# Four u parts, three dense PSUM banks, single PV banks, ScalarE copies and a new ordering model in a two-layer attention and token-MLP kernel

## The chip, the cores and the metric

The kernel runs on one core of one Trainium2 chip. The metric is the device time of one execution in microseconds (us), lower is better; a time quoted is the median of several executions. Each run has a state, fast or slow; ratios below use fast runs alone.

Engine names: PE is TensorE (matmuls; PEld its weight loads), DVE is VectorE, ACT is ScalarE, POOL is GpSimd, SP issues DMAs. L802 is line 802 of the kernel that the line belongs to. Lines shift between kernels, so the same code is L643 in one and L672 in another.

## The reference, cut to what matters

Two equal layers. Each is sliding-window attention (2048 tokens, 32 heads of 16, window 256) and then an MLP across tokens (2048 to 1792 and back), both with LayerNorm and a residual.

```python
x = A_x
for layer in range(2):                      # unrolled in the original
    x = x + attention(layernorm(x))         # softmax over the last 256 keys; qkv and output projection
    h = layernorm(layernorm(x))             # x is [tokens, 512]
    u = gelu(w1.T @ h + b1)                 # [1792, 512], contraction over all 2048 tokens
    x = x + w2.T @ u + b2
```

The contraction of u runs over tokens. So u can be accumulated in token parts of 512, as soon as attention has finished a part. The next layer's first matmuls need y = w2.T @ u, hence all of u.

## The kernel before

The kernel is a graph of operations. A greedy scheduler written in Python orders it before the launch: it keeps a model of time for each engine, always places the operation that can start first, and so fixes the instruction order of every engine. Operations carry a cost and a latency to their readers. PSUM (in the kernel 8 banks of 128x512 fp32) is a pool with a limit for each class: "sc" for scores, "small" for dense groups and PV results during attention.

```python
class Graph:
    def op(self, eng, fn, reads=(), writes=(), cost=100.0, lat=60.0, ...):  # 60 ns to any reader
    ...
    def _pick(self, e, cand, ready, free, mode):
        ...
        for o in cand:
            t = max(ready[o.idx], free)
            if e == "tensor" and o.mode != mode:
                t += SWITCH                        # 95 ns
            ...   # while a PV result is due within HOLD, no dense group may take a small bank
    HOLD = 1500.0
    WINDOW = {0: 250.0, 1: 150.0}                  # a score (0) or PV (1) goes first if it can start this soon
    def schedule(self):
        ...
        o.end = free[e] = m + o.cost
        o.done = o.end + o.lat                     # 200 ns for PE operations, also towards PE itself
        ...
        ready[u.idx] = max(ready.get(u.idx, 0.0), o.done)
```

```python
psum = Pool("psum", 8, {"sc": 6, "small": 2, "big": 6})
...
# in attention: five pieces for each of 4 head groups; a piece needs two score pairs (4 banks)
sa, sb_ = Tile(psum, 2, "sc"), Tile(psum, 2, "sc")
...                                                # scores on PE, exp on ACT (two 128x1024), mask on DVE
tO = Tile(psum, 2, "small")                        # PV result: a pair of banks
...
op("vector", f_ev, ...)                            # cs <- both banks, one copy of 128x1024
...
# in qkv: every copy out of PSUM (xhT, qT, stg, vt) is on "vector"
...
prepare(0, "big"); prepare(1); tos[0] = attention(0, ...); prepare(2); wo_block(0, tos[0])
tos[1] = attention(1, ...); prepare(3); wo_block(1, tos[1]); u_part([0, 1], True, False)
tos[2] = attention(2, ...); wo_block(2, tos[2]); u_part([2], False, False)
tos[3] = attention(3, ...); wo_block(3, tos[3], "big"); u_part([3], False, True)
```

`prepare` makes LayerNorm, q, k and v of a token part and, in the second layer, first the y blocks of the first. `wo_block` is the output projection with the LayerNorms that follow.

The softmax here doesn't subtract the row's maximum and nothing guards it: scores larger than these inputs give would overflow.

## Time and profile before

The time was 535.56 us (three runs, 534.03 to 537.4). From the page of the kernel before: the engines (busy us, share of the span, instructions) and the busy tenths in 40 equal slices; PEclk is the granted TensorE clock in tenths.

```profile
span 536.2 us, 15441 instructions
...
PE 443.4 (83%) x6754; PEld 208.6 (39%) x6816; DVE 375.9 (70%) x726; ACT 307.0 (57%) x340; POOL 135.1 (25%) x205
...
PE   2979767687688789899989878888779899699997
...
ACT  0555698888999810421784997588767921051000
...
PEclk9979998897999999999999999999988999989999
...
```

No engine is busy all the time.

ACT's timeline of the kernel before around its holes (start us, length us, then the work; in brackets the idle time before it and what ended it):

```profile
...
26.92 7.01 ACT L655 ACTIVATE pt<-PS 128x1024 bf16<-128x1024 f32 x8 [0.51 <-PE PS L643]
42.81 7.11 ACT L655 ACTIVATE pt<-PS 128x1024 bf16<-128x1024 f32 x8 [8.88 <-PE PS L688]
56.65 1.94 ACT L655 ACTIVATE pt<-PS 128x1024 bf16<-128x1024 f32 x2 [6.73 <-PE PS L688]
```

Three lines of PE's timeline near the end of the second layer: u of part 2 (L802), 14 matmuls of the last output projection (L763), then a 5.07 us hole until LayerNorm has made `xh_sb`, and u of part 3, with the clock cold at first (granted 0.50 from 467.6 to 474.4 us).

```profile
...
448.98 12.46 PE L802 MATMUL PS<-xh_sb,w1b 128*128 128x512 bf16 x55
461.27 3.19 PE L763 MATMUL PS<-wo_sb,oT 128*128 128x512 bf16 x14
469.52 14.65 PE L802 MATMUL PS<-xh_sb,w1b 128*128 128x512 bf16 x55 [5.07 <-DVE xh_sb L516]
...
```

The copy of PV results (DVE, 30 of 128x1024):

```profile
...
L731 DVE COPY cs<-PS 128x1024 f32<-128x1024 f32 x30 | 36.4, 1217 | 3.0 <-PE PS L688 2.7
...
```

### The profile page before, as it was taken

The numbers are of one execution on the slowest core, as the hardware profiler recorded it, in microseconds if no ns is written. First come the engines' busy times: TensorE is split into PE (matmuls) and PEld (weight loads), VectorE is DVE, ScalarE is ACT, GpSimd is POOL, SyncE is SP. The second block draws the span as 40 slices with busy tenths as digits, with TensorE's granted clock in tenths as the row PEclk, the third lists the DMA queues.
The fourth block names the chain that finished last, engine by engine and source line by source line (L and its number), as shares of the span: only waits on it lengthen the run. The fifth ranks groups of instructions, "written<-read, shape, count | busy, mean of one in ns | idle before, by whom it ended". The sixth has DMA issues, their size and how long they took to land.

```text
span 536.2 us, 15441 instructions
## 1 busy us (share of the span) xinstructions
PE 443.4 (83%) x6754; PEld 208.6 (39%) x6816; DVE 375.9 (70%) x726; ACT 307.0 (57%) x340; POOL 135.1 (25%) x205
## 2 busy tenths in 40 slices
PE   2979767687688789899989878888779899699997
PEld 1453432252233334344434335334434334244443
DVE  5889977786866678757789778778785657862322
ACT  0555698888999810421784997588767921051000
POOL 3525244343300120013203502712551020100000
PEclk9979998897999999999999999999988999989999
DMA  8912253242356543442255353156314662323663
GB/s 276 221 44 82 73 188 111 90 111 90 123 159 189 178 120 101 122 121 70 70 173 168 127 151 126 42 164 180 123 42 132 200 191 82 96 60 87 179 190 114
DMA packets 91435, 69.23 MB, mean 129 GB/s; under 512 B 16232, under 2 KB 79848, under 8 KB 91368
## 3 DMA queue, kind: packets, MB, share of 16 engines
q1 hardware_dynamic: 91368, 68.25, 42.8%
q8 instruction: 53, 0.87, 0.7%
q14 instruction: 14, 0.11, 0.1%
HBM read 49.42 MB, written 18.32 MB: 126 GB/s over the span
## 4 chain that ended last, share of the span: by engine, by line
PE 41%; ACT 27%; DVE 21%; issue 3%; POOL 3%; DMA 3%; SPq 0%; POOLq 0%; DVEq 0%
ACT pt L655 27%; PE PS L825 13%; PE PS L802 12%; PE PS L564 4%; PE PS L688 4%; PE PS L643 3%; DVE stats L505 3%; DVE cs L731 3%; PE PS L763 2%; DVE x_sb L767 2%; DVE pt L671 2%; DVE pt L668 2%; DVE xh_sb L516 2%; DVE stg L572 1%; PE PS L589 1%
## 5 line engine op out<-in xcount | busy, mean ns | idle before, releaser
L655 ACT ACTIVATE pt<-PS 128x1024 bf16<-128x1024 f32 (+1 forms) x304 | 280.9, 1041 | 104.0 <-PE PS L643 74.5
L802 PE MATMUL PS<-xh_sb,w1b 128*128 128x512 bf16 x431 | 107.4, 393 | 13.5 <-DVE xh_sb L516 6.7
L825 PE MATMUL PS<-ub,w2b 128*128 128x512 bf16 x428 | 101.7, 380 | 2.4 <-issue 1.3
L643 PE MATMUL PS<-qT,kbd 32*128 32x64 bf16 (+4 forms) x1632 | 62.8, 247 | 40.9 <-ACT pt L655 21.7
L671 DVE TENSOR_TENSOR pt<-pt,ldm 128x1024 bf16<-128x1024 bf16 (+1 forms) x80 | 57.2, 716 | 25.5 <-ACT pt L655 25.5
L564 PE MATMUL PS<-xhT,wqkv 128*128 128x512 bf16 x238 | 65.3, 404 | 8.1 <-DVE x_sb L767 1.5
L753 POOL TENSOR_TENSOR oT<-md 128x512 bf16<-128x512 f32 x30 | 41.2, 1375 | 111.0 <-DMA md<-rscr 111.0
L802 PEld LDWEIGHTS PS<-xh_sb,w1b 128*128 128x128 bf16 x448 | 41.2, 100 | 68.4 <-issue 10.5
L643 PEld LDWEIGHTS PS<-qT,kbd 32*128 32x128 bf16 x1632 | 23.8, 93 | 101.2 <-ACT pt L655 64.7
L825 PEld LDWEIGHTS PS<-ub,w2b 128*128 128x128 bf16 x448 | 40.7, 98 | 50.0 <-issue 5.2
L575 POOL TENSOR_SCALAR kbd<-stg,par 128x512 bf16<-128x512 bf16 x64 | 47.8, 758 | 48.8 <-DVE stg L572 48.6
L668 DVE TENSOR_TENSOR pt<-pt,ldm 128x512 bf16<-128x512 bf16 (+1 forms) x104 | 43.5, 428 | 20.2 <-ACT pt L655 19.8
L830 DVE SCALAR_TENSOR_TENSOR x_sb<-PS,b2col,x_sb 128x512 bf16<-128x512 f32 x32 | 23.0, 739 | 43.7 <-PE PS L825 43.7
L510 POOL TENSOR_SCALAR rstd<-agg 128x2 f32<-128x2 f32 (+1 forms) x36 | 9.2, 254 | 160.5 <-DVE agg L507 158.0
L817 ACT ACTIVATE ub<-ub,b1col 128x512 bf16<-128x512 f32 x28 | 18.6, 713 | 50.6 <-DVE ub L814 50.5
L814 DVE TENSOR_TENSOR ub<-PS,ub 128x512 f32<-128x512 f32 x56 | 35.9, 684 | 14.8 <-PE PS L802 14.8
L688 PE MATMUL PS<-pt,vt 64*18 64x64 bf16 (+4 forms) x3040 | 38.7, 242 | 7.5 <-DVE pt L668 2.3
L505 DVE BATCH_NORM_STATS2 stats<-x_sb 128x6 f32<-128x512 bf16 x64 | 42.6, 684 | 3.2 <-DMA x_sb<-in_A_x_dram 2.6
L731 DVE COPY cs<-PS 128x1024 f32<-128x1024 f32 x30 | 36.4, 1217 | 3.0 <-PE PS L688 2.7
L763 PE MATMUL PS<-wo_sb,oT 128*128 128x512 bf16 x121 | 34.6, 403 | 4.7 <-DVE oT L719 3.1
L564 PEld LDWEIGHTS PS<-xhT,wqkv 128*128 128x128 bf16 x256 | 22.3, 102 | 40.2 <-issue 8.9
L688 PEld LDWEIGHTS PS<-pt,vt 64*18 64x18 bf16 x3040 | 30.3, 84 | 18.4 <-ACT pt L655 5.3
(45 smaller groups left out, 316.0 us busy)
## 6 DMA issues: line engine op xcount, KB each, us to landing
scr<-cs SPq DMA_DIRECT2D x30, 512.0 KB, 3.5
w1b<-in_B_w_dram SPq DMA_DIRECT2D x56, 256.0 KB, 3.0
w2b<-in_B_w_dram SPq DMA_DIRECT2D x16, 896.0 KB, 5.9
md<-scr SPq DMA_DIRECT2D x60, 128.0 KB, 2.6
md<-rscr SPq DMA_DIRECT2D x60, 128.0 KB, 3.4
out_dram<-x_sb SPq DMA_DIRECT2D x16, 128.0 KB, 4.7
wqkv<-in_A_wqkv_dram SPq DMA_DIRECT2D x3, 512.0 KB
x_sb<-in_A_x_dram SPq DMA_DIRECT2D x3, 512.0 KB, 9.3
```

Of the source, the lines that this page charges most:

```text
L505: op("vector", lambda e, t=t: e.bn_stats(stats[:, t, :], x_sb[:, t, :]), reads=[f"x{t}"], writes=[f"st{t}"], cost=dve_cost(512))
L564: mm_group(ft, 4, lambda e, c: e.matmul(PS[:, ft.slot, :], lhsT=wqkv[:, c, which * 512 + o * P:which * 512 + (o + 1) * P], rhs=xhT[:, tx.s ...
L575: op("gpsimd", lambda e, h=h: e.tensor_scalar(kbd[:, tk[o].slot, :, h, :], stg[:, ts.slot, :].rearrange("p (s n) -> p s n", n=64), par[:, ...
L643: last = e.matmul(PS[:, bank(r), c0 * 64:(c0 + nb) * 64], lhsT=kbd[32 * r:32 * r + 32, tkk.slot, jj, :, :].rearrange("p h n -> p (h n)"), ...
L655: return e.activation(pt[:, tp.slot, 2 * u:2 * u + 2, 0:n], PS[:, b0:b0 + 2, 0:n], ACTF.Exp, scale=SMSCALE)
L668: return e.tensor_tensor(v, v, msk.unsqueeze(1).to_broadcast([P, 4, w]), op=ALU.mult)
L671: return e.tensor_tensor(v, v, msk.unsqueeze(1).unsqueeze(1).to_broadcast([P, 4, k, w]), op=ALU.mult)
L688: last = e.matmul(PS[32 * r:32 * r + 18, tO.slots[h], q0 * 64:(q0 + nb) * 64], lhsT=vt[64 * h:64 * h + 64, tvv.slot, jj, 4 * o + r, :], rh ...
L731: return e.tensor_copy(cs[:, tc.slot], PS[:, b0:b0 + 2, :])
L763: mm_group(ft, 4, lambda e, o, i=i, ft=ft: e.matmul(PS[:, ft.slot, :], lhsT=oT[:, tos[o][0].slot, i * P:(i + 1) * P], rhs=wo_sb[:, 4 if to ...
L802: out_ = e.matmul(PS[:, tu.slot, :], lhsT=w1b[:, tw.slot, s, tt * P:(tt + 1) * P], rhs=xh_sb[:, 4 * m + s, :], start=(n == 0 and s == 0), ...
L825: mm_group(ft, NFT, lambda e, fc: e.matmul(PS[:, ft.slot, :], lhsT=w2b[:, tw.slot, fc, k * P:(k + 1) * P], rhs=uT(fc), start=(fc == 0), st ...
```

## The change

The intent: more dense matmuls available for PE while ACT does exponentials (u in four parts, in the first layer only; a third dense bank), less work for DVE early (ScalarE may take the copies of token parts 0 and 1), PV banks handled one by one, and an ordering model that was meant to be closer to the chip, with a clock gate. (The gate is the rule inside the model, by which PE costs double in some stretches.) Cut to its core:

```diff
+STEPS = ("p0 p1 a0 p2 w0 u0 a1 p3 w1 u1 a2 w2 u2 a3 w3 U3",     # first layer: four u parts
+         "p0 p1 a0 p2 w0 a1 p3 w1 u01 a2 w2 u2 a3 w3 U3")       # second layer: block order as before
...
+    LAT = {"tensor": 200.0, "vector": 120.0, "scalar": 150.0, "gpsimd": 100.0, "sync": 60.0}
...
-            t = max(ready[o.idx], free)
+            t = free
             if e == "tensor" and o.mode != mode:
                 t += SWITCH
+            t = max(ready[o.idx], t)
...
-    HOLD = 1500.0
-    WINDOW = {0: 250.0, 1: 150.0}
+    HOLD = 0.0
+    WINDOW = {0: 100.0, 1: 150.0}
...
+                if e == "tensor":
+                    o.cost = self._clocked(m, o.cost)    # twice the cost where the model takes the clock for half
-                o.done = o.end + o.lat
+                o.done = o.end + (o.lat if o.lat is not None else self.LAT[e])
-                ready[u.idx] = max(ready.get(u.idx, 0.0), o.done)
+                ready[u.idx] = max(..., o.end if e == "tensor" and "tensor" in u.engs else o.done)
...
-        psum = Pool("psum", 8, {"sc": 6, "small": 2, "big": 6})
+        psum = Pool("psum", 8, {"sc": 6, "small": 3, "big": 6})
...
+                if m < NACT:                              # NACT = 2, both layers
+                    engs["scalar"] = (lambda e: e.copy(dst(), src()), act_cost(512))
...
-                tO = Tile(psum, 2, "small")
+                tO = [Tile(psum, 1, "small") for _ in range(2)]
...
-                op("vector", f_ev, reads=[tO], writes=[tc], cost=dve_cost(1024, psum=True), prio=-1e5)
+                for h in range(2):
+                    op("vector", ... e.tensor_copy(cs[:, tc.slot, h], PS[:, tO.slot, :]) ..., cost=dve_cost(512, psum=True))
```

Two costs in the model changed as well (LayerNorm scaling 320, the POOL multiply 1680). A switch that was never used (`apart`) went out.

## The prediction

> **What bounds the kernel now.** No single engine: PE is busy 83%, DVE 70%, ACT 57% of 536.2 us (engine table); the chain of waits is PE 41%, ACT 27%, DVE 21%. By stages (10 us windows):
>
> - 20-60 us, first layer: DVE is busy 38 of 40 us with PSUM copies, LayerNorm, masks. ACT, which owes the exponentials, has holes at 33.9-42.8 and 49.9-56.7 us.
> - 60-190 us: ACT is busy 116 of 130 us with exponentials (1052 ns each for 128x1024). PE is busy only 75%: dense work has run out. The u matmuls (L802) start at 144 us, since u of token parts 0 and 1 is one block after the second output projection.
> - 187-230 us: exponentials are over; PE does most of u of part 2 (until 218 us), the last output projection, then u of part 3.
> - 230-440 us, second layer: PE 80-90% busy, because y of the first layer fills it; a 5.1 us PE hole at 464 us before the last u.
> - 484-532 us: y, dense, untouched.
>
> The granted clock is half in stretches (27-37, 82-85, 102-106, 122-130, 399-406, 467-475 us), some 34 us in all; at 469 us an L802 matmul shows 634 ns instead of 379. [...]
>
> **What the change does.**
>
> 1. First layer's u in four parts: the 56 matmuls of part 0 (0.219 us spacing in dense stretches, 12 us) can run from about 105 us, in the holes and cold clock of the exponential stage. Price: 14 more DVE adds of 684 ns, 9.6 us. Some 10 us of u leave 187-219 us; the last projection and LayerNorm chain stays, about 20 us by my estimate. Net gain 6-9 us.
> 2. Early copies may go to ScalarE: up to 64 (token parts 0 and 1, both layers). DVE pays 0.41-0.68 us each. I expect 20-40 to move, at 0.6 us (Ln of 128x512 from PSUM takes 600 ns). At 20-60 us, 12-16 moved copies take 7-10 us off the saturated DVE: 5-8 us gained. In the second layer PE is the limit: 1-3 us.
> 3. PV banks copied singly: two copies near 0.68 us replace one of 1217 ns, 30 x 0.15 = 4 us more DVE work, mostly hidden; a bank comes free about 0.6 us earlier. PE waited 8.2 us for this copy, plus 14.1 us at weight loads: 2 us gained.
> 4. A third dense bank overlaps dense evacuation, but leaves score pairs five banks at times. About zero.
> 5. Order by the clock model: fewer half-clock windows in the first layer. 2-4 us. The hole at 464 us may stay, since the second layer keeps its block order.
>
> DMA bytes and the y stage stay. The terms overlap; sum some 16 us.
>
> **Prediction:** 519 us, 8 in 10 between 506 and 533. Chances: faster by over 2% 0.68, within 2% 0.28, slower 0.04.
>
> **What the profile would show.** Copies on ACT before 60 us and its two holes halved; last exponential of the first layer near 180 us, not 187; L802 from about 105 us; y starting near 218, not 230 us; mean clock at least 0.97; 60 cs copies; DVE busy near 370 us, ACT near 325. The second layer shortens by only 3-6 us.
>
> **What would make it wrong.** DVE becoming the limit at 105-190 us through the extra adds; ACT copies landing between exponentials where ACT is the limit; the third dense bank starving scores (ACT waiting for L643 more than 74.5 us); cold windows falling elsewhere. Better than predicted: the new order closing the second layer's holes too.

The five terms as they stand add up to 16 to 26 us (6-9, 5-8 and 1-3, 2, 0, 2-4). The 2 to 4 us of term 5 are the author's estimate: no trace shows what order does to the granted clock. The "about 20 us" of term 1 can be checked: in the trace of before, the last output projection of the first layer goes on at 199.50 us and u of part 3 starts at 219.52 us.

## More of the kernel before

The stages show more. The next answer gives the busy time of each engine in stretches: 20 us to 60 us; to the last exponential of the first layer (187.4 us); to its last gelu (231.3 us); to the first exponential of the second layer (251.0 us); to its last (432.1 us); to the last gelu (485.8 us), after which only y is left. The columns after the engines are the granted clock, the DMA share and GB/s.

```profile
...
core 0: us, PE busy (x) PEld busy (x) DVE busy (x) ACT busy (x) POOL busy (x), PEclk, DMA share, GB/s
20.00:60.00 40.00, 33.70 (x504) 19.72 (x508) 38.12 (x95) 22.67 (x27) 17.47 (x27) 0.91 0.36 100
60.00:187.40 127.40, 94.55 (x2332) 44.18 (x2346) 94.37 (x161) 116.18 (x126) 38.39 (x47) 0.95 0.44 136
187.40:231.30 43.90, 39.72 (x279) 18.00 (x284) 34.54 (x67) 11.65 (x18) 4.78 (x9) 1.00 0.42 116
231.30:251.00 19.70, 19.49 (x111) 9.11 (x112) 11.18 (x24) 1.30 (x2) 4.54 (x11) 1.00 0.38 105
251.00:432.10 181.10, 152.80 (x2972) 72.27 (x2995) 139.47 (x269) 140.34 (x152) 57.12 (x76) 0.98 0.42 128
432.10:485.80 53.70, 46.25 (x299) 20.13 (x302) 35.65 (x65) 11.93 (x18) 4.92 (x9) 0.94 0.34 97
...
```

Until 60 us DVE is full (38.1 of 40 us) and ACT is not (22.7). To 187 us ACT is full (116.2 of 127.4 us) and PE is not (94.6). In the second layer's exponential stage (251 to 432 us) PE is busy 152.8 of 181.1 us, so 28.3 us of it are idle.

From the groups by line in 251 to 432 us of the kernel before, the score matmuls (after the second bar: idle time of PE just before them, with what ended it):

```profile
...
L643 PE MATMUL PS<-qT,kbd 32*128 32x320 bf16 (+4 forms) x808 | 30.5, 244 | 16.1 <-ACT pt L655 9.3 <-DVE cs L731 2.0 <-POOL kbd L575 0.9
...
```

And three lines of PE's timeline within that stage (L825 is y):

```profile
...
306.73 0.40 PE L643 MATMUL PS<-qT,kbd 32*128 32x128 bf16 x12 [0.46 <-ACT pt L655]
307.06 1.04 PE L825 MATMUL PS<-ub,w2b 128*128 128x512 bf16 x4
...
400.95 2.34 PE L802 MATMUL PS<-xh_sb,w1b 128*128 128x512 bf16 x5 [1.78 <-ACT pt L655]
...
```

PE stood idle before score matmuls, 9.3 us in this stage, until an exponential had freed their banks. Dense work existed: at 307.06 us y comes right behind such scores, with no wait of its own. Not every hole is of that kind: at 400.95 us a dense matmul of u, L802, waited 1.78 us for an exponential itself, so there a free bank was missing too.

## The result, and the profile after

The kernel after took 503.1 us (three runs, 501.5 to 506.04). Ratios here are the mean time of one kernel's fast runs over that of the other's of the same rounds, so not quite the ratio of the quoted medians. The ratio to before is 0.940 (95% interval 0.932 to 0.948): faster, as forecast, but by 32 us instead of 16, and outside the stated range. The page of the kernel after:

```profile
span 499.8 us, 15471 instructions
...
PE 430.5 (86%) x6746; PEld 209.0 (42%) x6816; DVE 377.1 (75%) x745; ACT 321.9 (64%) x365; POOL 137.0 (27%) x205
...
PE   2998758798859859699999899898889998999997
...
ACT  1788987898789961080598998697988872070000
...
PEclk9999988899979979899999999999999999999999
...
```

Its stages, cut at the same events (last exponential of the first layer at 182.4 us, last gelu 223.1, first exponential of the second layer 242.3, last 410.7, last gelu 450.0):

```profile
...
core 0: us, PE busy (x) PEld busy (x) DVE busy (x) ACT busy (x) POOL busy (x), PEclk, DMA share, GB/s
20.00:60.00 40.00, 35.18 (x686) 20.38 (x688) 39.23 (x97) 36.00 (x46) 17.49 (x24) 1.00 0.50 144
60.00:182.40 122.40, 93.18 (x2143) 44.76 (x2156) 101.00 (x185) 107.00 (x115) 39.12 (x50) 0.92 0.43 136
182.40:223.10 40.70, 34.63 (x244) 15.88 (x249) 27.65 (x49) 12.63 (x18) 3.16 (x5) 0.90 0.34 99
223.10:242.30 19.20, 19.09 (x108) 8.96 (x109) 12.28 (x24) 2.97 (x5) 4.74 (x11) 1.00 0.39 108
242.30:410.70 168.40, 154.50 (x3003) 74.88 (x3034) 140.42 (x278) 144.63 (x159) 58.22 (x76) 1.00 0.47 146
410.70:450.00 39.30, 36.36 (x267) 17.24 (x271) 32.29 (x62) 11.97 (x18) 4.81 (x9) 1.00 0.36 101
...
```

| stretch | before, us | after, us | gained, us |
|---|---|---|---|
| start to last exponential, first layer | 187.4 | 182.4 | 5.0 |
| to last gelu, first layer | 43.9 | 40.7 | 3.2 |
| to first exponential, second layer | 19.7 | 19.2 | 0.5 |
| to last exponential, second layer | 181.1 | 168.4 | 12.7 |
| to last gelu, second layer | 53.7 | 39.3 | 14.4 |
| y to the end | 50.4 | 49.8 | 0.6 |

The profiled runs differ by 36.4 us, the medians by 32.5. The first layer gained 8.2 us, where the prediction had 11 to 17 us from its first two terms. The second layer, whose block order the change leaves as it was, gained 28.2 us, where it had 3 to 6. That is more than the whole miss. (One stretch of this table needs care: of the 14.4 us after the last exponential of the second layer, about 7 are luck of the order of before, see "Luck of the order".)

In the second layer's exponential stage PE is busy about the same time as before (154.5 and 152.8 us) but in 168.4 us instead of 181.1: its idle time fell from 28.3 to 13.9 us (some records of matmuls are missing in both traces, 62 of 6816 before and 70 after, so PE's idle time is a little too high in both). The score matmuls of that stage, to compare with the line of before:

```profile
...
L672 PE MATMUL PS<-qT,kbd 32*128 32x320 bf16 (+4 forms) x808 | 29.7, 243 | 3.1 <-DVE qT L567 1.1 <-DVE vt L567 1.0 <-POOL kbd L604 0.7
...
```

Idle time before them fell from 16.1 to 3.1 us. What the profile puts down to exponentials fell from 9.3 us to nothing listed. At the end of the second layer, the lines that answer to the three of before:

```profile
...
419.20 2.54 PE L791 MATMUL PS<-wo_sb,oT 128*128 128x512 bf16 x11 [1.29 <-DVE oT L748]
...
422.87 11.39 PE L830 MATMUL PS<-xh_sb,w1b 128*128 128x512 bf16 x51
...
438.41 4.49 PE L830 MATMUL PS<-xh_sb,w1b 128*128 128x512 bf16 x19 [1.13 <-DVE xh_sb L541]
...
```

Here 11 matmuls of the last projection (L791) come before the 51 of u (L830). LayerNorm is done while those run, the hole is 1.13 us instead of 5.07, and the clock stays up (granted 1.00 over the stretch, where before had 0.94). (Before with one constant of its model moved by 2 ns loses that hole as well: 1.46 us.) The end of the first layer of the same kernel still has the poor order, projection after u, with a hole of 4.87 us:

```profile
...
193.10 7.07 PE L830 MATMUL PS<-xh_sb,w1b 128*128 128x512 bf16 x31
200.00 3.19 PE L791 MATMUL PS<-wo_sb,oT 128*128 128x512 bf16 x14
208.06 7.97 PE L830 MATMUL PS<-xh_sb,w1b 128*128 128x512 bf16 x30 [4.87 <-DVE xh_sb L541]
```

The ScalarE copies (25 of 64 moved) and the PV copies of the kernel after, from the groups by shape (busy us, mean ns):

```profile
...
L569 ACT COPY xhT<-PS 128x512 bf16<-128x512 bf16 x8 | 4.5, 590 | 19.2 <-PE PS L579 19.2
...
L569 ACT CAST qT<-PS 128x512 bf16<-128x512 f32 x7 | 4.1, 585 | 1.7 <-PE PS L595 1.7
L569 ACT CAST vt<-PS 128x512 bf16<-128x512 f32 x5 | 3.0, 598 | 0.0
L569 ACT CAST stg<-PS 128x512 bf16<-128x512 f32 x5 | 3.0, 592 | 3.6 <-PE PS L595 3.6
...
```

```profile
...
L759 DVE COPY cs<-PS 128x512 f32<-128x512 f32 x60 | 38.5, 682 | 6.4 <-PE PS L717 6.2
...
```

### The profile page after: what moved, and what is told of

The parts are those of the page before. It is cut to its first block, busy times and chain, and to the rows that moved or that the text cites. A ratio compares the mean times of both kernels' runs of the same rounds, so it can differ in the third digit from the quotient of the medians.

```text
span 499.8 us, 15471 instructions
## 1 busy us (share of the span) xinstructions
PE 430.5 (86%) x6746; PEld 209.0 (42%) x6816; DVE 377.1 (75%) x745; ACT 321.9 (64%) x365; POOL 137.0 (27%) x205
## 4 chain that ended last, share of the span: by engine, by line
PE 50%; DVE 27%; ACT 9%; DMA 7%; POOL 2%; issue 2%; SPq 1%; POOLq 0%
PE PS L830 16%; PE PS L853 15%; ACT pt L684 9%; PE PS L717 5%; PE PS L595 5%; DVE stats L530 4%; PE PS L672 4%; DVE pt L700 3%; DVE xh_sb L541 3%; DVE pt L697 3%; DMA rr<-cs 3%; DVE cs L759 3%; PE PS L791 2%; DMA rscr<-rr 2%; DVE vt L567 2%
## 5 line engine op out<-in xcount | busy, mean ns | idle before, releaser
L830 PE MATMUL PS<-xh_sb,w1b 128*128 128x512 bf16 x423 | 103.8, 387 | 17.2 <-DVE xh_sb L541 7.7
L781 POOL TENSOR_TENSOR oT<-md 128x512 bf16<-128x512 f32 x30 | 39.3, 1309 | 154.9 <-DMA md<-rscr 154.8
L700 DVE TENSOR_TENSOR pt<-pt,ldm 128x1024 bf16<-128x1024 bf16 (+1 forms) x80 | 58.0, 726 | 16.2 <-ACT pt L684 16.1
L830 PEld LDWEIGHTS PS<-xh_sb,w1b 128*128 128x128 bf16 x448 | 40.4, 99 | 68.0 <-DVE xh_sb L541 13.4
L595 PE MATMUL PS<-xhT,wqkv 128*128 128x512 bf16 x239 | 62.5, 393 | 5.4 <-issue 2.8
L604 POOL TENSOR_SCALAR kbd<-stg,par 128x512 bf16<-128x512 bf16 x64 | 50.0, 792 | 36.8 <-DVE stg L567 30.5
L842 DVE TENSOR_TENSOR ub<-PS,ub 128x512 f32<-128x512 f32 x70 | 47.3, 688 | 10.5 <-PE PS L830 10.1
L717 PE MATMUL PS<-pt,vt 64*18 64x64 bf16 (+4 forms) x3040 | 42.1, 257 | 7.0 <-ACT pt L684 2.5
L759 DVE COPY cs<-PS 128x512 f32<-128x512 f32 x60 | 38.5, 682 | 6.4 <-PE PS L717 6.2
L717 PEld LDWEIGHTS PS<-pt,vt 64*18 64x18 bf16 x3040 | 32.6, 89 | 19.5 <-ACT pt L684 10.7
L541 DVE TENSOR_SCALAR xh_sb<-x_sb,agg,rstd 128x512 bf16<-128x512 bf16 x64 | 28.5, 476 | 8.8 <-POOL rstd L537 8.5
L791 PE MATMUL PS<-wo_sb,oT 128*128 128x512 bf16 x121 | 30.9, 381 | 3.7 <-DVE oT L748 1.3
```

The source lines that it names most:

```text
L595: mm_group(ft, 4, lambda e, c: e.matmul(PS[:, ft.slot, :], lhsT=wqkv[:, c, which * 512 + o * P:which * 512 + (o + 1) * P], rhs=xhT[:, tx.s ...
L604: op("gpsimd", lambda e, h=h: e.tensor_scalar(kbd[:, tk[o].slot, :, h, :], stg[:, ts.slot, :].rearrange("p (s n) -> p s n", n=64), par[:, ...
L700: return e.tensor_tensor(v, v, msk.unsqueeze(1).unsqueeze(1).to_broadcast([P, 4, k, w]), op=ALU.mult)
L717: last = e.matmul(PS[32 * r:32 * r + 18, tO[h].slot, q0 * 64:(q0 + nb) * 64], lhsT=vt[64 * h:64 * h + 64, tvv.slot, jj, 4 * o + r, :], rhs ...
L759: op("vector", lambda e, tO=tO[h], tc=tc, h=h: e.tensor_copy(cs[:, tc.slot, h], PS[:, tO.slot, :]), reads=[tO[h]], writes=[(tc, h)], cost= ...
L830: out_ = e.matmul(PS[:, tu.slot, :], lhsT=w1b[:, tw.slot, s, tt * P:(tt + 1) * P], rhs=xh_sb[:, 4 * m + s, :], start=(n == 0 and s == 0), ...
```

## The experiments

Theory O, for order: the miss is the ordering model. Rival R: the miss is resources, that is, ScalarE copies and banks. As the answers came, two more questions arose: do bank and model work only together, and how much of any number is luck of the greedy order? All kernels gave correct results. "The model" below is the ordering model without the hold; "banks" means the third dense bank, the single PV banks and the hold of 0 together. The hold was never changed alone. "Undone" means one part of the change taken back from after; "only" means the part added to before. Differences are given as differences of ratios to before (each measured on the same chip in the same rounds), times 536 us. The ratio of after was measured in three orders, see "Luck of the order" below: 0.940, 0.933, 0.933, mean 0.9353. That mean is what the undone parts are set against.

### The ordering model alone, and all but it

The edit of the first is the ordering part of the diff above, put on before (hold and pair stay); the second is its reverse on after:

```diff
-    LAT = {"tensor": 200.0, "vector": 120.0, "scalar": 150.0, "gpsimd": 100.0, "sync": 60.0}
+    LAT = {"tensor": 60.0, "vector": 60.0, "scalar": 60.0, "gpsimd": 60.0, "sync": 60.0}
-    WINDOW = {0: 100.0, 1: 150.0}
+    WINDOW = {0: 250.0, 1: 150.0}
-                if e == "tensor":
-                    o.cost = self._clocked(m, o.cost)
...   # also o.done towards PE again, SWITCH added after the wait, the two old costs
```

> The kernel before with only the ordering model of after (latencies per engine, clock gate, no 200 ns between dependent PE groups, score window 100 ns, two costs); blocks, banks, copies and the 1500 ns hold stay. Theory O (the order from the truer model is what the prediction undersized; PE's waits of score matmuls for exponentials vanish): 515 to 522 us, PE score waits on ACT well below the 21.7 us of before, most of the gain in the second layer. Rival R (resources: ACT copies and a third dense bank made the second layer dense): 530 to 537 us.

> The kernel after with the ordering model of before (60 ns latencies, no clock gate, 200 ns between dependent PE groups, score window 250 ns, old costs; hold stays 0); four u parts, ScalarE copies, third bank, single PV banks stay. Theory O: 515 to 522 us, with PE waiting for ACT at scores again near 20 us in total. Rival R: 503 to 508 us.

Measured: model only 529.12 us, ratio 0.980 (0.973 to 0.987), a gain of 11 us and less than theory O expected. Its profiled run fell in the slow state, so its stages are not compared. All but the model: 523.55 us, ratio 0.973, so undoing the model costs 20 us. The order matters, but it isn't the whole. Neither theory alone fits. The profile of all but the model is a fast one. Its first layer ends at 223.5 us, as in after; the 20 us are all in the second layer, 8.1 in the exponential stage (176.5 against 168.4 us) and 9.8 after it (49.1 against 39.3 us). The mechanism that theory O named did not show: score matmuls waited for exponentials 12.6 us over both layers, not near 20 (before 21.7, after 9.1), and PE idled 13.6 us in that exponential stage, as little as in after (13.9); the stage is longer because it has more work in it (PE busy 162.9 us against 154.5).

### No ScalarE copies

```diff
-    NACT = 2
+    NACT = 0
```

> The kernel after with no ScalarE copies (NACT 0). My size for this part: 6 to 11 us, so 509 to 514 us, lost almost wholly before 60 us of the first layer, where DVE is full. Rival R: over 515 us, lost in the second layer too.

Measured: 519.41 us, ratio 0.966; the part is worth 16 us here. The stretch 20 to 60 us of this kernel, in the columns of the stage tables:

```profile
...
20.00:60.00 40.00, 32.55 (x490) 16.09 (x492) 39.12 (x96) 21.69 (x26) 13.68 (x22) 0.99 0.41 113
...
```

With the same DVE load (39.1 us of 40) ACT gets 21.7 us of work done instead of 36.0. So the mechanism was as predicted, DVE is what held ACT back. The size was not: the total is over 515 us and part of the loss is in the second layer, as the rival had it. The first layer ended at 231.1 us instead of 223.1, the second took 285.6 us instead of 276.7. Of the latter, 7.1 us lie in the stretch after the last exponential (46.4 against 39.3 us).

### Two dense banks

```diff
-        psum = Pool("psum", 8, {"sc": 6, "small": 3, "big": 6})
+        psum = Pool("psum", 8, {"sc": 6, "small": 2, "big": 6})
```

> The kernel after with two instead of three dense banks (PV banks still single). Predicted worth of the third bank was about zero: 500 to 506 us. Rival R (the third bank lets dense matmuls run on while banks are copied): 512 us or more, with PE dense lines waiting for DVE copies.

Measured: 517.38 us, ratio 0.960, so the third bank is worth 13 us. The second layer took 297.1 us against 276.7, while the first was done at 216.2 us, no later than after's. In the second layer's exponential stage the wait for exponentials is back:

```profile
...
L672 PE MATMUL PS<-qT,kbd 32*128 32x320 bf16 (+4 forms) x808 | 29.9, 244 | 11.6 <-ACT pt L684 8.6 <-DVE x_sb L858 1.4 <-DVE cs L759 0.8
...
```

But that stage is only 3 us longer than in after (171.3 against 168.4 us). Its PE idles 23.7 us instead of 13.9, and it gets 62 u matmuls done in it instead of 88. They are left for the stretch after the last exponential, which takes 14 us more than in after (columns of the stage tables):

```profile
...
409.60:462.80 53.20, 48.10 (x316) 21.50 (x314) 39.45 (x70) 12.59 (x17) 4.92 (x9) 0.97 0.38 108
...
```

There the poor order at the end of the layer is back as well, with a hole of 4.88 us, so up to 4 of the 14 us need not be the bank's.

### The third bank in the second layer only

```diff
-                if q[0] + c > q[1]:
+                if q[0] + c > q[1] - (tl.cut if tl.cls == "small" else 0):   # cut is 1 in the first layer
```

> After with the third dense bank allowed in the second layer only (two dense banks in the first). The run with two dense banks in both layers was done with the first layer at 216 us (after: 223) and lost 20 us in the second. Theory B (the third bank earns its time in the second layer, where y groups of 14 matmuls hold a bank while single PV banks and short dense groups need others): 495 to 501 us, faster than after, PE idle at second-layer scores waiting for exponentials under 2 us. Rival C (chance of the greedy order: what two banks gained in the first layer was luck tied to the rest): 503 to 515 us.

Measured: 503.17 us, ratio 0.937, no better than after. Theory B falls: the first layer of "two dense banks" and the second layer of after, each the better one, don't add up to a faster kernel. Nor does the total lose anything without the third bank in the first layer. Its profiled run was slow, so nothing is read from its stages.

### PV in a pair of banks

```diff
-                tO = [Tile(psum, 1, "small") for _ in range(2)]
+                tO = Tile(psum, 2, "small")
...
-                for h in range(2):
-                    op("vector", ... cs[:, tc.slot, h] ... 512 ...)
+                op("vector", ... cs[:, tc.slot] <- PS[:, tO.slot:tO.slot + 2, :] ..., cost=dve_cost(1024, psum=True))
```

> After with the PV result again in a pair of banks and one 128x1024 copy. If single banks matter (a pair must be free at once among three dense banks): 510 to 518 us, with dense work unable to run beside it. If only the third bank and the model matter: 500 to 506 us, DVE busy about 2 to 4 us less.

Measured: 494.03 us, ratio 0.921: faster than after, against both expectations. Taking back this part of the change helps.

### The old block order

```diff
-            for step in STEPS[layer].split():
+            for step in STEPS[1].split():
```

> After with the first layer in the old block order (u of parts 0 and 1 as one block). Prediction: worth 6 to 9 us, all in the first layer, so 509 to 512 us with 14 fewer DVE adds; second layer within 2 us of that of after. If the part is worth nothing: 501 to 506 us.

Measured: 509.83 us, ratio 0.951, so the four parts are worth 9 us in total. The place was not as expected: the second layer took 283.8 us (after 276.7), although nothing of its blocks had changed; the first 221.4 (after 223.1). Of the 7.1 us lost in the second layer, 5.9 lie after the last exponential (45.2 against 39.3 us), where the projection again came after u, with a hole of 4.87 us. A part that shifts time where it isn't is a sign of luck in the order, which runs below measure.

### One piece of the model

```diff
-            t = free
+            t = max(ready[o.idx], free)
             if e == "tensor" and o.mode != mode:
                 t += SWITCH
-            t = max(ready[o.idx], t)
...
-                ... o.end if e == "tensor" and "tensor" in u.engs else o.done)
+                ... o.done)
```

> After with one piece of the ordering model undone: a PE group that follows its own predecessor on PE counts as ready 200 ns late again, and the mode switch is added after the wait, not beside it. If this piece carries the model's worth (about 20 us of after were lost with the whole model undone): 512 to 522 us, in the second layer. If latencies and the score window carry it: 502 to 508 us.

Measured: 514.59 us, ratio 0.959: this piece is worth 13 of the model's 20 us. The other pieces except the clock gate (latencies, score window, two costs) were not run apart. Its second layer took 291.9 us, with the wait for exponentials back:

```profile
...
L671 PE MATMUL PS<-qT,kbd 32*128 32x320 bf16 (+4 forms) x808 | 30.9, 249 | 9.7 <-ACT pt L683 6.4 <-DVE cs L758 1.7 <-DVE agg L531 0.6
...
```

Why it works was not measured apart. The reading that fits: with 200 ns between two halves of one dense accumulation, the model believes that a dense group leaves gaps, and it orders PE's queue for gaps that aren't there (in the trace of after, the 51 matmuls of u from 422.87 us start 0.22 us apart on average, with no such gap).

### Luck of the order

```diff
-SWITCH = 95.0
+SWITCH = 97.0        # and 93.0
```

> After with one constant of the ordering model moved by 2 ns (mode switch 97 instead of 95): same instructions, another greedy order. It measures how much of a time is luck of the order. If the orders are stable: 501 to 505 us. If luck is large: off by 5 us or more, and differences below that of single undone parts mean nothing.

> After with the mode switch at 93 ns, the second sample of the luck of the order. Stable: 501 to 505 us; else off by 5 us or more.

> Before with the mode switch at 97 ns: was the order of before an unlucky one? If yes, 520 to 530 us; if 535.6 us is typical of its construction, 532 to 540 us.

Measured: after 499.54 us (ratio 0.933) and 499.92 us (0.933), before 531.25 us (0.992). The same instructions in another greedy order differ by 3 to 4 us (by 5 us in the last experiment below). Differences of 13 us or more between single orders are therefore beyond it, one of 9 us only just, those of 3 us aren't. In stages luck is larger, up to 7 us: after's first layer ended at 223.1, 216.1 and 218.9 us. The second layer is steadier, 276.7, 280.3 and 278.6 us for after against 304.9 and 298.5 us for before; in none of after's three orders does the profile list a wait for exponentials among the first three releasers of its score matmuls' idle time.

The two orders of before split the second layer's gain into a firm and a soft part. Its exponential stage took 181.1 and 182.0 us, with 28.3 us of PE idle time in both; after's three orders took 168.4, 168.0 and 171.1 us, with 13.9 to 16.4 us idle. That gain, about 12 us, is there in every order drawn. The stretch from the last exponential to the last gelu took 53.7 and 46.6 us in before, and 39.3, 40.7 and 38.7 us in after: here 7 of the 14.4 us in the table above are bad luck of before. Between the means of the orders the second layer gained 23 us (301.7 to 278.5) and the first 11 (230.7 to 219.4).

### Model and banks, without copies and u parts

```diff
-    NACT = 2
+    NACT = 0
-            for step in STEPS[layer].split():
+            for step in STEPS[1].split():
```

> After without ScalarE copies and without the four u parts: only the new ordering model, single PV banks, no hold and the third dense bank are left of the change. Theory I (model and third bank work only together, and they make the second layer dense): second layer 281 to 288 us of the 305 of before, first layer like that of before (228 to 234), total 512 to 520 us, PE idle at second-layer scores waiting for exponentials under 4 us. Rival R (ScalarE copies are needed for the second layer's gain): second layer over 292 us, total over 523 us.

Measured: 518.27 us, ratio 0.968. First layer 232.4 us, about as before; second layer 285.4 us, so 19.5 of the 28.2 us in this one order; rival R falls. The exponential stage has 8.6 of the 19.5 us and the stretch after it 11.3, the soft part; the others together lost 0.5. The score matmuls of its second exponential stage:

```profile
...
L672 PE MATMUL PS<-qT,kbd 32*128 32x320 bf16 (+4 forms) x808 | 30.2, 243 | 4.5 <-ACT pt L684 2.0 <-DVE stg L567 0.8 <-DVE ub L839 0.8
...
```

### Banks alone

The kernel of the last experiment with the ordering model undone, by the edit shown above.

> Before with only the bank part: third dense bank, single PV banks copied one by one, no hold; ordering model, copies and block order of before. It completes the square with before (second layer 304.9 us), the model alone (299.4) and both (285.4). Theory I (the two work only together): second layer 298 to 306 us, total 527 to 538 us. Rival (the banks alone do it): second layer under 291 us, total under 523 us.

Measured: 527.58 us, ratio 0.988; second layer 292.0 us. The total is in the range of theory I, the second layer isn't. (The 299.4 us that this expectation gives for the model alone came from the slow profile and shouldn't have been used.) By totals the square is: model 2.0%, banks 1.2%, both 3.2%. They add, within intervals of 0.6 to 0.8% each; "only together" is wrong. The wait of the score matmuls for exponentials fell by steps:

```profile
...
L669 PE MATMUL PS<-qT,kbd 32*128 32x320 bf16 (+4 forms) x808 | 29.7, 243 | 9.8 <-ACT pt L681 4.0 <-issue 2.0 <-DVE cs L756 1.0
...
```

It is 9.3 us before, 4.0 with the banks, 2.0 with banks and model, and not listed in after. It is a poor measure of time, though: the exponential stage takes 171.8 us with the banks, no longer than the 172.6 us with banks and model, and the last run of all has 4.3 us of this wait in a stage of 166.2 us. What the ordering model does within that stage therefore stays open: beside the banks alone it gained nothing there, but taken from after it cost 8.1 us.

### Without the clock gate in the model

```diff
-                if e == "tensor":
-                    o.cost = self._clocked(m, o.cost)
```

> After with the ordering model's clock gate taken out (PE costs at full clock), rest of the model kept. If the clock gate carries the model's worth: 515 to 523 us. If the 200 ns and the latencies carry it (undoing the former alone cost 11 us): within the luck of the order, 498 to 508 us.

Measured: 501.11 us, ratio 0.936, the same as after. The clock gate in the ordering model earned nothing that could be measured.

### The pair form in two more orders

> PV in a pair of banks with one copy, mode switch 97 ns. If the pair is truly the better form (30 copies of about 1.2 us in place of 60 of 0.68 us): 491 to 498 us like the first order of it (494.0). If that order was lucky: 498 to 506 us, no better than after's three orders (499.5 to about 503).

> As before it, with 93 ns: the third order of the pair form. Truly better: 491 to 498 us; luck: 498 to 506 us.

Measured: 495.49 us (ratio 0.926) and 493.10 us (0.922). With the first, the mean is 0.923 against 0.935 for three orders of after: the single PV banks cost about 6.5 us. The pair form beats both kernels in all its orders. The two orders also show how the end of a layer falls out. With 97 ns, 13 matmuls of the last projection (L790) go before the 55 of u:

```profile
...
413.81 2.97 PE L790 MATMUL PS<-wo_sb,oT 128*128 128x512 bf16 x13 [1.32 <-DVE oT L748]
416.62 12.25 PE L829 MATMUL PS<-xh_sb,w1b 128*128 128x512 bf16 x55
...
433.01 4.49 PE L829 MATMUL PS<-xh_sb,w1b 128*128 128x512 bf16 x19 [1.12 <-DVE xh_sb L541]
...
```

With 93 ns, 14 of them go after 51 of u, and the hole is 4.87 us:

```profile
...
408.38 11.39 PE L829 MATMUL PS<-xh_sb,w1b 128*128 128x512 bf16 x51
419.61 3.19 PE L790 MATMUL PS<-wo_sb,oT 128*128 128x512 bf16 x14
427.66 5.30 PE L829 MATMUL PS<-xh_sb,w1b 128*128 128x512 bf16 x12 [4.87 <-DVE xh_sb L541]
...
```

From last exponential to last gelu that is 38.8 us against 45.2 us. A change of 2 ns in a constant decides it.

The PV copy of the pair form, to compare with that of after: 36.5 us against 38.5 us of DVE, so 2 us, too little to be all of the 6.5.

### A pair with two copies

```diff
 # pair of banks as above, but
+                for h in range(2):
+                    op("vector", ... cs[:, tc.slot, h] <- PS[:, tO.slots[h], :] ..., cost=dve_cost(512, psum=True))
```

> The PV result again in an aligned pair of banks, but copied by two 128x512 copies as in after. In after, 18 of the 30 PV results lie across two pairs of banks (counted in the program), so that they keep two pairs from the scores. If that placement is what single PV banks cost: 491 to 497 us, like the three orders of the pair with one copy. If the second copy itself costs the 6 us: 498 to 504 us.

> The same with the mode switch at 97 ns, a second order, since one order says little within 3 us. Placement: 491 to 497 us; second copy: 498 to 504 us.

Measured: 497.69 us (ratio 0.923) and 504.05 us (0.933; one of four runs slow). One order lies with the pair, the other with after. So it isn't settled whether the placement across pairs or the second copy costs the time; with a luck of up to 5 us it would take more orders of each.

## Why the prediction was wrong

The direction was right (0.68 for faster by over 2%). The size was not: 519 us forecast, 506 the lower end, 503.1 measured. Point by point:

1. **u in four parts, 6 to 9 us.** The number agrees, 9 us, but the agreement may be luck. The first u matmuls moved from 144 us to before 100 us. That the gain lies in the first layer wasn't shown: the run without the parts ended that layer at 221.4 us, within the three orders of after (216.1 to 223.1), and lost 7.1 us in the second layer, 5.9 of them where 2 ns decide.
2. **ScalarE copies, 5 to 8 us in the first layer and 1 to 3 in the second.** Right mechanism, wrong size. 25 copies moved at 585 to 598 ns, ACT did 36.0 instead of 22.7 us of work by 60 us, and the holes of 8.88 and 6.73 us are gone. The term measured 16 us when undone. Its 8 us in the first layer are the forecast, measured from one order of after; from the other two they would be 12 and 15. Most of the rest appears after the last exponential of the second layer, where the order decides.
3. **PV banks singly, 2 us gained.** Wrong sign: about 6.5 us lost. The DVE cost was small as forecast (38.5 against 36.4 us). In after, 18 of the 30 PV results lie across two pairs of banks (counted in the program); in before none. Whether that is the cause is open.
4. **Third dense bank, "about zero".** Wrong: 13 us, all in the second layer, since with two banks fewer u matmuls fit between the scores (62 instead of 88) and the rest came after the last exponential. The prediction feared that scores would starve (ACT waiting for scores over 74.5 us). That wait fell to 43.0 us.
5. **Order by the new model, 2 to 4 us through fewer cold windows in the first layer.** Wrong in size, place and cause: 11 us alone on before, 20 us when taken from after, and about 10 of the 20 lie in the stretch after the last exponential, where luck of the order is 7 us. The clock gate contributes nothing measurable; the dropped 200 ns between PE operations, with the switch overlapping the wait, is worth 13 us.
6. **"The second layer shortens by only 3 to 6 us."** This is the step that failed. It rested on "PE 80-90% busy" in 10 us slices, read as a PE limit. The stage of 181.1 us held 28.3 us of PE idle time, and the 53.7 us after it another 7.5, and 6.8 us of half clock. In after the stage has 168.4 us with 13.9 us idle, and the second layer shortened by 28.2 us (23 between the means of the orders), not 3 to 6. Work that waited also stood in front of work that didn't: at 306.73 us PE stood idle 0.46 us for scores that waited for an exponential, while matmuls of y, which had no wait of their own, came after them in the queue. That one more bank puts such work in the gaps is shown by PE's idle time in the stage: 13.9 to 16.4 us in after's three orders, 23.7 in the one order with two dense banks. That the new order does so isn't: without one piece of the model it is 23.4 us, but without the whole model 13.6. The prediction looked for what the change does to the second layer's blocks, saw that they stay, and stopped. But order and banks act on every stage. Its list of what would make it wrong did name "the new order closing the second layer's holes too"; that came true, though the hole at 464 us closed by luck.

The undone parts sum to 20 + 13 + 16 + 9 - 6.5 = 51.5 us, more than the 35 us by which the mean of after's three orders (ratio 0.9353) beats before. So they overlap, as the square of model and banks did not. What is shown, in one order each: the second layer's gain comes from model and banks for 19.5 of 28.2 us. The rest, 8.7 us, goes with copies and u parts together, which brought the exponential stage from 172.6 to 168.4 us and the stretch after it from 42.4 to 39.3 us. How much of that is luck of the order isn't known.

The stretches of half clock were read right, but for the first, which begins at 30.7 us and not at 27. In the trace of before the granted clock is 1.0 or 0.5; its six stretches of 0.5 between 30 and 475 us last 3.4 us (from 81.9 and 102.3 us) or 6.8 us (from 30.7, 122.8, 399.3 and 467.6 us), 34.1 us in all, and a last one is cut short by the end. Matmuls of 128x512 showed 634 ns there and 379 ns at full clock; in a row they started 427 and 216 ns apart. What makes the clock fall was not shown. Only one of the six falls came in a hole of 5.07 us; in the 8 us ahead of the other five, PE's longest idle time was 1.02 to 1.78 us. In the 3.4 us ahead of the six falls PE was busy for 0.30 us (at 467.6 us) to 1.66 us (at 399.3 us).

## What to carry to other kernels

An engine that is 84% busy in a stage of 181 us leaves up to 28 us to win (14 of them were won here): ask what ends each idle time before calling it the limit, above all where work that waits stands in the queue in front of work that does not (at 306.73 us for 0.46 us; in all PE idled 9.3 us of the stage before scores that waited for exponentials). Before judging one part of a change to a list-scheduled kernel, perturb the order with a meaningless constant a few times: here 3 to 5 us of a total and up to 7 us of a stage were luck. Single undone parts of 13 to 20 us could be told from it, one of 9 us hardly, one of 6 us only with three orders of each. From here the next steps are to keep the pair of PV banks (493 to 495 us) and to put the last projection ahead of u at the end of each layer, which the kernel now does by luck in one layer and not in the other (a hole of 1.13 against 4.87 us); the latter wasn't run.
